# Heads in pairs on the contraction axis, and sread computed transposed

## The chip, the cores and the metric

The kernel runs on one core of a Trainium2 chip. The metric is device time in microseconds (us), lower is better. The core has five engines that run side by side, each through its own list of instructions in order: TensorE (PE in the profile, its weight loads PEld), VectorE (DVE), ScalarE (ACT), GpSimd (POOL) and SyncE (SP). POOL and SP start the DMA transfers here; the profile calls POOL's queue q0 and SP's queue q1.

## The reference

Cross attention between a long sequence x and 32 state rows, both ways, per batch and head, and then a feed-forward layer over all rows (B = 8 batches, H = 8 heads, S = 512, Ns = 32, D = 64, d_model = 512, d_ff = 2048):

```python
scores  = softmax(scale * x @ state^T)      # [B, H, 512, 32]
xread   = scores @ state                    # [B, H, 512, 64]
scores2 = softmax(scale * state @ x^T)      # [B, H, 32, 512]
sread   = scores2 @ x                       # [B, H, 32, 64]
x2 = concat([xread, sread], rows) -> [B * 544, H * D]
h  = x2 @ w_in
out = (h * sigmoid(h)) @ w_out              # float32 [4352, 512]
```

The inputs are float32; the kernel works in bf16 and sums in float32.

## The kernel before

Both softmaxes use the same exponentials, without a maximum: `exps` writes exp_nat = exp(scale * x state^T), with 128 sequence rows on the partitions and, in the free dimension, c (4 rows per partition), 4 heads ("slots") and 32 state rows. `norm` sums over the 32 on DVE, takes the reciprocal and multiplies on POOL (tile an). The xread rows are never formed: since xread @ w_in = a @ (state @ w_in), the kernel builds W1 = state @ w_in per head (`w1_cols`, L330) and G1 (L356) multiplies W1 with the transposed weights aT. ACT applies SiLU to the result (tile g, L377), and G2 (L385) multiplies g with w_out, 16 matmuls (ft) for each of four output blocks (tt). The sread rows of all batches are collected and put through w_in and w_out at the end as a ninth batch (L366, L385, L407).

Loading. x of a batch is [head, 512 rows, 64]. `fetch_x` loads it with one cast DMA from POOL (L99), partition p holding rows 4p to 4p+3 of each head: runs of 4 rows, 1 KB read and 512 B written in bf16. x_nat has ten blocks: block 0 and block 9 are ones, 1 to 8 are the heads. Two x_nat buffers exist, so the load of batch n+2 has to wait until sread of batch n has read its buffer. `transpose_x` (L111) makes xT by a DMA transpose from SP's queue; batches 0 and 1 use PE instead (`pe_transpose_x`, L187). The weights come in ten cast DMAs on POOL's queue (L116, L119), the state of batches 1 to 7 in one on the same queue (L200, tile st_b), issued after batch 0's norm. It is copied twice side by side (st_n, L462), transposed by PE in 16 pieces (L213) and evicted to stT in four copies.

Scores. The 128 contraction rows of one matmul hold two of the four c for one head. stT holds, for each head, a block of state for the upper and one for the lower 64 rows, with zeros elsewhere. A matmul has xT as the stationary operand and writes 2 x 32 columns (L238); a half batch (hg, four heads) takes 8 matmuls. The result is ordered slot, c, n, so `exps` reads it permuted.

Sread. `sread(b, hg)` (L289) takes exp_nat as stationary operand and five blocks of x_nat, four heads and the ones, as the moving one: 4 matmuls of 320 columns (L293). Only the diagonal blocks are of use, and the ones column gives the sum. DVE takes the reciprocal of one column (L302) and scales four 32x64 blocks into s_nat (L306). After batches 3 and 7 `transpose_s` turns s_nat into xmT by a DMA transpose.

Order of the work. It is written out by hand. In the loop for batch b = 1 to 7 the next batch n = b + 1 is prepared at fixed places (tt, ft) between the G2 matmuls: scores and exps of n at (0, 10) (at (0, 12) for b = 1), norm and the DMA transposes of a at (0, 14), sread at (1, 6) and (1, 13), `transpose_x(n + 1)` at (2, 12), W1 at (2, 8) and (3, 4), `load_x(n + 2)` at (3, 0). The first G1 of batch n stands at (3, 1). A DMA of POOL or SP starts as soon as its queue reaches it and its waits are met, whatever place it has between the matmuls. Batch 0 is different: its first part runs while weights and state arrive, with sread(0) at ft 8 and 9, the state at ft 3 to 5, the four column chunks of W1 at ft 0, 2, 6 and 10, and the PE transposes of x(1) at ft 14.

On SP the order per batch is: the two transposes of a, two stores, the transpose of x, two stores. PSUM: two banks each for G2 and G1, and four (a0 to a3, taken in turn by `bank`) for everything else.

Of the kernel before, what the change touches and what calls it, by code (L numbers as in the profile page):

```python
# [8 lines left out]
FP32 = mybir.dt.float32  # L9
BF16 = mybir.dt.bfloat16  # L10
# [7 lines left out]
B = 8  # L18
H = 8
# [10 lines left out]

HEAD_OF_SLOT = [[0, 1, 2, 3], [5, 4, 7, 6]]
# [3 lines left out]
def kernel(  # L35
# [15 lines left out]

    xpool = ctx.enter_context(tc.tile_pool(name="xpool", bufs=2))
    xtpool = ctx.enter_context(tc.tile_pool(name="xtpool", bufs=3))
# [18 lines left out]
    st_b = pers.tile([128, 16, D], BF16)  # L72
    st_n = pers.tile([128, 16, 2, D], BF16)
    st0_f = pers.tile([128, 2, D], FP32)
    st0_n = pers.tile([128, 2, 2, D], BF16)

    stT = pers.tile([128, B, H, 2, NS], BF16)
    w_in_sb = pers.tile([128, 4, DF], BF16)
    w_out_sb = pers.tile([128, NFT, DM], BF16)
    s_nat = pers.tile([128, 2, DM], BF16)  # L80
# [11 lines left out]
    def new_x(b):  # L92
        t = xpool.tile([128, 10, 4, D], BF16, tag="x_nat", name=f"x_nat{b}")
        x_nat[b] = t
        nc.gpsimd.memset(t[:, 0, :, :], 1.0)
        nc.gpsimd.memset(t[:, 9, :, :], 1.0)

    def fetch_x(b):
        nc.gpsimd.dma_start(  # L99
            x_nat[b][:, 1:9, :, :],  # L100
            x[b].rearrange("h (p c) d -> p h c d", p=128, c=4),
        )
# [5 lines left out]
    def transpose_x(b):  # L108
        t = xtpool.tile([128, 16, 128], BF16, tag="xT", name=f"xT{b}")
        xT[b] = t  # L110
        nc.sync.dma_start_transpose(  # L111
            t[:], x_nat[b][:, 1:9, :, :].rearrange("p h c d -> p (h c d)")
        )
# [14 lines left out]
    def keep_busy(n, pool, tag):  # L128
# [11 lines left out]
    nc.sync.dma_start(  # L140
        st0_f[:], state[0].rearrange("(g h) n d -> (h n) g d", g=2)
    )
# [7 lines left out]
    nc.vector.memset(stT[:, 1:8], 0.0)  # L150
    make_identity(nc, ident)
    new_x(0)
# [10 lines left out]
    for u in range(2):  # L163
        copy(nc.vector, st0_n[:, :, u, :], st0_f[:])
    ps0 = bank([128, 2, 4, NS], BF16, "ps_st0")
    for hg in range(2):
        nc.tensor.transpose(ps0[:, hg, :, :], st0_n[:, hg, :, :], ident[:])
    for u, eng in enumerate((nc.vector, nc.scalar)):
        copy(
            eng,  # L170
            stT[ds(64 * u, 64), 0, :, u, :],
            ps0[ds(64 * u, 64), :, :, :].rearrange("p g h n -> p (g h) n"),
        )
    keep_busy(3, psH, "h1")
# [4 lines left out]
    def pe_transpose_x(b, hg, nb=2, new=bank, engs=(nc.vector, nc.scalar)):  # L179
        if b not in xT:  # L180
            xT[b] = xtpool.tile([128, 16, 128], BF16, tag="xT", name=f"xT{b}")
        m = 8 // nb
        for u in range(nb):
            ps = new([128, m, 128], BF16, "ps_xt")
            for i in range(m):
                j = m * u + i
                nc.tensor.transpose(  # L187
                    ps[:, i, :],
                    x_nat[b][:, 1 + 4 * hg + j // 2, ds(2 * (j % 2), 2), :],
                    ident[:],  # L190
                )
            copy(engs[u], xT[b][:, ds(8 * hg + m * u, m), :], ps[:])

    copy(nc.vector, x_nat[0][:, 1:5, :, :], x_f[:, 0:4, :, :])
    pe_transpose_x(0, 0, 2, lambda sh, dt, nm: psO.tile(sh, dt, tag="o", name=nm))
    copy(nc.vector, x_nat[0][:, 5:9, :, :], x_f[:, 4:8, :, :])


    def load_state():
        nc.gpsimd.dma_start(  # L200
            st_b[:],
            state.rearrange("b h n d -> (b h n) d").rearrange("(p k) d -> p k d", k=16),
        )

    stT_v = stT.rearrange("p b h c (n2 k) -> p c b h n2 k", n2=2)
# [3 lines left out]
    def transpose_state(half):  # L209
        ps = bank([128, 8, B, H, 2], BF16, "ps_st")  # L210
        st_ps[half] = ps
        for kk in range(8):
            nc.tensor.transpose(  # L213
                ps[:, kk, :, :, :], st_n[:, 8 * half + kk, :, :], ident[:]
            )

    def evict_state(half, u, eng):
        dst = stT_v[
            ds(64 * u, 64), u, ds(1, 7), :, :, ds(8 * half, 8)
        ].rearrange("p b h n k -> p (b h) n k")  # L220
        src = st_ps[half][ds(64 * u, 64), :, ds(1, 7), :, :].rearrange(
            "p k b h n -> p (b h) n k"
        )
        copy(eng, dst, src)
# [7 lines left out]
    def scores(b, hg):  # L232
        ps = bank([128, 4, 4, NS], FP32, "ps_sc")
        sc_ps[hg] = ps
        for s in range(4):
            h = HEAD_OF_SLOT[hg][s]
            for cp in range(2):
                nc.tensor.matmul(  # L238
                    ps[:, s, ds(2 * cp, 2), :],
                    xT[b][:, 2 * h + cp, :],  # L240
                    stT[:, b, h, :, :],
                    start=True,
                    stop=True,
                    skip_group_check=True,
                )

    def exps(b, hg):
        e = att.tile([128, 4, 4, NS], BF16, tag="exp", name="exp_nat")
        exp_nat[b, hg] = e
        nc.scalar.activation(  # L250
            e[:],
            sc_ps[hg].rearrange("p s c n -> p c s n"),
            func=EXP,
            bias=0.0,
            scale=SCALE,
        )
# [32 lines left out]
    def sread(b, hg):  # L289
        e = exp_nat[b, hg]  # L290
        ps = bank([128, 5, D], FP32, "ps_sr")
        for c in range(4):
            nc.tensor.matmul(  # L293
                ps[:],
                e[:, c, :, :],
                x_nat[b][:, ds(5 * hg, 5), c, :],
                start=(c == 0),
                stop=(c == 3),
                skip_group_check=True,
            )  # L300
        rb = att.tile([128, 1], FP32, tag="rb", name="rb")
        nc.vector.reciprocal(rb[:], ps[:, 0 if hg == 0 else 4, 0:1])  # L302
        for s in range(4):
            h = HEAD_OF_SLOT[hg][s]
            blk = h + 1 - 5 * hg
            nc.vector.tensor_scalar(  # L306
                s_nat[ds(32 * (b % 4), 32), b // 4, ds(64 * h, 64)],
                ps[ds(32 * s, 32), blk, :],
                rb[ds(32 * s, 32), :],
                None,  # L310
                op0=MULT,
            )

    def transpose_s(q):
        nc.sync.dma_start_transpose(xmT[:, q, :, :], s_nat[:, q, :])
# [3 lines left out]
    def w1_cols(b, cols, engs):  # L319
        pss = {}  # L320
        if b not in W1:
            W1[b] = wpool.tile([128, 2, DF], BF16, tag="W1", name="W1")
        for f, n in cols:
            for hg in range(2):
                pss[f, hg] = bank([128, 512], FP32, "ps_w1")
            for s in range(4):
                for hg in range(2):
                    h = HEAD_OF_SLOT[hg][s]
                    r = 64 * (h % 2)
                    nc.tensor.matmul(  # L330
                        pss[f, hg][ds(32 * s, 32), 0:n],
                        stT[ds(r, 64), b, h, h % 2, :],
                        w_in_sb[ds(r, 64), h // 2, ds(f, n)],
                        start=True,
                        stop=True,
                        tile_position=(r, 32 * s),
                        skip_group_check=True,
                    )
        for f, n in cols:
            for hg in range(2):  # L340
                copy(engs[hg], W1[b][:, hg, ds(f, n)], pss[f, hg][:, 0:n])
# [95 lines left out]
    load_state()  # L437
# [17 lines left out]
    for ft in range(NFT):  # L455
# [4 lines left out]
        if ft == 3:  # L460
            for u in range(2):
                nc.vector.tensor_copy(st_n[:, :, u, :], st_b[:])  # L462
        if ft == 4:
            transpose_state(0)
            transpose_state(1)
            evict_state(0, 0, nc.vector)
            evict_state(0, 1, nc.vector)
            evict_state(1, 0, nc.vector)
        if ft == 5:
            evict_state(1, 1, nc.scalar)  # L470
        if ft in (8, 9):
            sread(0, ft - 8)
# [25 lines left out]
    for ft in range(NFT):  # L498
        if ft == 5:
            w1_chunks(1, (3,), (nc.scalar, nc.scalar))  # L500
        if ft == 9:
            sread(1, 0)
# [4 lines left out]
        if ft == 13:  # L507
            sread(1, 1)
            load_x(3)
# [6 lines left out]
    for b in range(1, B):  # L516
        n = b + 1
        lead = 4 if b == 1 else 6
        for tt in range(4):
            for ft in range(NFT):  # L520
# [3 lines left out]
                if n < B:  # L524
# [9 lines left out]
                    if at == (1, 6):  # L534
                        sread(n, 0)
                    if at == (1, 13):
                        sread(n, 1)
                        if n == 3:
                            transpose_s(0)
                        if n == 7:  # L540
                            transpose_s(1)
                    if at == (2, 12):
                        if n + 1 < B:
                            transpose_x(n + 1)
                    if at == (3, 0):
                        if n + 2 < B:
                            load_x(n + 2)
# [46 lines left out]
```

## Time and profile before

| | us |
|---|---|
| median of 3 runs | 236.28 (234.55, 236.28, 240.29) |
| the profiled execution, its own time | 236.61 |
| its span, first to last instruction | 234.70 |
| batch period in the middle (e.g. 77.7 to 101.8) | 24.07 |
| the period with the longest wait for aT (125.84 to 152.30) | 26.46 |

The span in 40 slices (one slice is 5.9 us) shows the load of each engine and of the DMA engines in tenths:

```profile
PE   7698899999989999999999959999999999999970
...
DVE  6626456702721183108410822136212721100110
ACT  3753669797287928691879257763977297544110
...
PEclk9999999999999999999999999999999999999996
...
DMA  6999991970493039603990296106410421110111
GB/s 194 182 209 204 204 137 50 185 129 3 55 226 125 0 46 199 182 0 47 185 174 0 45 186 130 45 3 160 110 45 3 113 89 47 45 44 36 57 26 63
```

A 9 for PE is a slice in which it has work nearly all the time; the low slices are the start, slice 24 (135 to 141 us) and the end. In the first five slices the DMA engines are full: weights, state and x(1) arrive. Of the two queues, q0 carries the casting loads of POOL, q1 the stores, the transposes and the first loads of SP. The row for PE in a slice says nothing of what it waits for; that is read from the chain and the waits. The clock granted to PE is full but for the end.

### The profile page before, as it was taken

What the parts mean: (1) busy time and instruction counts of PE and PEld (TensorE: products, weight loads), DVE (VectorE), ACT (ScalarE), POOL (GpSimd) and SP (SyncE); (2) the same over time, 40 slices, a digit from 0 to 9 for tenths busy, and PEclk for the clock granted to TensorE, in tenths of its full rate; (3) what the DMA queues carried; (4) which work ended last, traced back from release to release, by engine and by line L of the source; (5) the groups of instructions that cost most, each with busy time, mean ns of one, the idle gap of its engine ahead of it and who ended that gap; (6) DMA issues with size and microseconds to landing.
All of it is one profiled execution on the core that took longest, in us unless ns stands there. A gap on an engine that the chain in (4) does not pass through costs nothing.

```text
span 234.7 us, 3567 instructions
## 1 busy us (share of the span) xinstructions
PE 215.3 (92%) x1388; PEld 102.0 (43%) x1414; DVE 77.9 (33%) x184; ACT 141.2 (60%) x237; POOL 35.6 (15%) x56
## 2 busy tenths in 40 slices
PE   7698899999989999999999959999999999999970
PEld 2334335544434543444344424454345434566550
DVE  6626456702721183108410822136212721100110
ACT  3753669797287928691879257763977297544110
POOL 8670020400500050005000500021001200000000
PEclk9999999999999999999999999999999999999996
DMA  6999991970493039603990296106410421110111
GB/s 194 182 209 204 204 137 50 185 129 3 55 226 125 0 46 199 182 0 47 185 174 0 45 186 130 45 3 160 110 45 3 113 89 47 45 44 36 57 26 63
DMA packets 38637, 23.37 MB, mean 100 GB/s; under 512 B 21212, under 2 KB 34268, under 8 KB 38620
## 3 DMA queue, kind: packets, MB, share of 16 engines
q0 software_dynamic: 12192, 8.13, 25.8%
q1 hardware_dynamic: 26428, 15.01, 24.7%
q8 instruction: 11, 0.18, 0.3%
q14 instruction: 6, 0.05, 0.1%
HBM read 17.37 MB, written 8.91 MB: 112 GB/s over the span
## 4 chain that ended last, share of the span: by engine, by line
PE 68%; DMA 10%; ACT 8%; DVE 5%; issue 3%; POOL 1%; POOLq 0%; DVEq 0%
PE o L385 34%; DMA aT<-an 7%; DMA st_b<-in_state_dram 3%; PE ps_sr L293 3%; ACT g L377 2%; ACT L377 2%; PE ps_sc L238 2%; PE o_half L407 1%; DVE stT L125 1%; ACT exp_nat L250 1%; ACT o_sb L123 1%; POOL an L269 1%; DVE s_nat L306 1%; PE ps_xt L187 1%; DVE rs L266 1%
## 5 line engine op out<-in xcount | busy, mean ns | idle before, releaser
L385 PE MATMUL o<-w_out_sb,g 128*128 128x512 bf16 x488 | 135.0, 379 | 1.7 <-issue 0.8
L385 PEld LDWEIGHTS <-g 128*128 128x128 bf16 x528 | 49.8, 98 | 60.9 <-issue 10.6
L269 POOL TENSOR_TENSOR an<-exp_nat,rc 128x512 bf16<-128x512 bf16 (+1 forms) x16 | 15.9, 1008 | 131.6 <-DVE rc L267 131.6
L266 DVE TENSOR_REDUCE rs<-exp_nat 128x16 f32<-128x512 bf16 x16 | 10.6, 660 | 52.9 <-ACT exp_nat L250 52.9
L125 DVE COPY o_sb<-o 128x512 f32<-128x512 f32 x17 | 11.4, 669 | 46.3 <-PE o L385 46.3
L123 ACT ACTIVATE o_sb<-o 128x512 f32<-128x512 f32 x15 | 8.9, 597 | 29.3 <-issue 19.6
L306 DVE TENSOR_SCALAR s_nat<-ps_sr,rb 32x64 bf16<-32x64 f32 x64 | 18.0, 281 | 1.3
L250 ACT ACTIVATE exp_nat<-ps_sc 128x512 bf16<-128x512 f32 x16 | 8.8, 595 | 0.9 <-PE ps_sc L238 0.8
L293 PEld LDWEIGHTS <-exp_nat 128*128 128x128 bf16 x64 | 6.2, 98 | 5.2 <-ACT exp_nat L250 0.5
L366 PEld LDWEIGHTS <-w_in_sb 128*128 128x128 bf16 x64 | 6.3, 98 | 3.9
L250 ACT ACT_TABLE_LOAD x6 | 7.7, 1283 | 0.1
L377 ACT ACT_TABLE_LOAD x6 | 7.7, 1283 | 0.1
L330 PEld LDWEIGHTS <-stT 64*32 64x32 bf16 x264 | 2.8, 89 | 8.7 <-issue 8.5
L131 PE MATMUL ps_busy<-busy 128*128 128x512 bf16 x11 | 5.0, 584 | 1.3 <-DVE busy L148 1.2
L385 PE MATMUL o_a<-w_out_sb,g 128*128 128x512 bf16 x15 | 5.5, 379 | 0.1
L356 PEld LDWEIGHTS <-W_206 128*128 128x128 bf16 x32 | 2.8, 97 | 6.2 <-DVE W_206 L125 2.2
L356 PEld LDWEIGHTS <-W_2203 128*128 128x128 bf16 x32 | 3.1, 97 | 4.1 <-issue 0.8
L356 PEld LDWEIGHTS <-W_1932 128*128 128x128 bf16 x32 | 3.1, 97 | 4.1 <-issue 0.8
L356 PEld LDWEIGHTS <-W_1110 128*128 128x128 bf16 x32 | 3.1, 97 | 4.1 <-issue 0.8
L356 PEld LDWEIGHTS <-W_379 128*128 128x128 bf16 x32 | 3.1, 98 | 3.9 <-issue 0.3
L356 PEld LDWEIGHTS <-W_1384 128*128 128x128 bf16 x32 | 3.1, 98 | 3.8 <-issue 0.4
L356 PEld LDWEIGHTS <-W_835 128*128 128x128 bf16 x32 | 3.1, 98 | 3.7 <-issue 0.2
(520 smaller groups left out, 331.0 us busy)
## 6 DMA issues: line engine op xcount, KB each, us to landing
out_dram<-o_sb SPq DMA_DIRECT2D x33, 256.0 KB, 2.5
w_in_sb<-in_moe_w_in_dram POOLq DMA_DIRECT2D x3, 512.0 KB, 9.5
w_out_sb<-in_moe_w_out_dram POOLq DMA_DIRECT2D x3, 512.0 KB, 11.3
x_f<-in_x_dram SPq DMA_DIRECT2D x2, 512.0 KB, 4.7
w_in_sb<-in_moe_w_in_dram POOLq DMA_DIRECT2D x2, 256.0 KB, 6.8
w_out_sb<-in_moe_w_out_dram POOLq DMA_DIRECT2D x2, 256.0 KB, 7.2
x_nat_115<-in_x_dram POOLq DMA_DIRECT2D x1, 512.0 KB, 16.8
x_nat_225<-in_x_dram POOLq DMA_DIRECT2D x1, 512.0 KB, 5.8
```

Of the source, the lines that this page charges most:

```text
L123: nc.scalar.activation(dst, src, func=COPY, bias=0.0)
L125: eng.tensor_copy(dst, src)
L131: nc.tensor.matmul(ps[:], busy[:, 0:128], busy[:], start=True, stop=True, skip_group_check=True)
L250: nc.scalar.activation(e[:], sc_ps[hg].rearrange("p s c n -> p c s n"), func=EXP, bias=0.0, scale=SCALE,)
L266: nc.vector.tensor_reduce(rs[:], e[:], axis=AX, op=ADD)
L269: eng.tensor_tensor(a[:, ds(c, n)], e[:, ds(c, n)], rc[:, ds(c, n)].to_broadcast([128, n, 4, NS]), op=MULT,)
L293: nc.tensor.matmul(ps[:], e[:, c, :, :], x_nat[b][:, ds(5 * hg, 5), c, :], start=(c == 0), stop=(c == 3), skip_group_check=True,)
L306: nc.vector.tensor_scalar(s_nat[ds(32 * (b % 4), 32), b // 4, ds(64 * h, 64)], ps[ds(32 * s, 32), blk, :], rb[ds(32 * s, 32), :], None, op ...
L356: nc.tensor.matmul(ps[:], W1[b][:, hg, ds(128 * ft, 128)], aT[b][:, hg, :, :], start=(hg == 0), stop=(hg == 1), skip_group_check=True,)
L366: nc.tensor.matmul(ps[:, 0:256], w_in_sb[:, kt, ds(128 * ft, 128)], xmT[:, :, kt, :], start=(kt == 0), stop=(kt == 3), skip_group_check=True,)
L377: nc.scalar.activation(g[:, 0:n], ps[:, 0:n], func=SILU, bias=0.0)
L385: nc.tensor.matmul(outs[tt][:], gt[b * NFT + ft][:, ds(128 * tt, 128)], w_out_sb[:, ft, :], start=(ft == 0), stop=(ft == NFT - 1), skip_gr ...
```

## The change

Heads are taken in pairs on the contraction axis. x_nat becomes [partition, c, head, d] without the blocks of ones; a 128-row piece of xT then holds two heads of one c instead of two c of one head, and `exps` reads its scores in the order in which they lie. stT holds for each of the four head pairs two blocks of 32 columns; in heads 4 to 7 the two are swapped (`u ^ g`), which goes with HEAD_OF_SLOT in `w1_cols`.

- `fetch_x`: four DMAs, one for each c, with runs of 64 float32 (256 B) in memory, in place of one DMA with runs of 1 KB. x is loaded for batches 1 to 7 this way.
- State: seven float32 DMAs on SP's queue (runs of 256 B), two casts on DVE, 2 x 4 transposes, 2 x 4 evictions on DVE. A memset of one element on POOL, after batch 0's norm, holds the first of each group back.
- `sread(b)`: once per batch. A matrix of ones is the stationary operand of 8 matmuls over the exponentials (128 columns), which leaves the sums on all partitions; x_nat is the stationary operand of 16 matmuls (64 columns), which gives sread already transposed. DVE takes the reciprocal of 128 x 256 sums and multiplies four 64 x 64 pieces straight into xmT. s_nat and `transpose_s` go.
- Places: sread(0) from ft 8 and 9 to ft 3; sread(1) in one piece at ft 13; sread(n) from (1, 6) and (1, 13) to (1, 14); `load_x(n + 2)` from (3, 0) to (1, 14); `transpose_x(n + 1)` from (2, 12) to (1, 6). xtpool has two buffers instead of three.

In the new order SP has, per batch: the two transposes of a, one store, the transpose of x, three stores. On DVE the reciprocal and the four multiplies of sread(0) stand between the two casts of the state.

```diff
     def fetch_x(b):
-        nc.gpsimd.dma_start(
-            x_nat[b][:, 1:9, :, :],
-            x[b].rearrange("h (p c) d -> p h c d", p=128, c=4),
-        )
+        x_re = x[b].rearrange("h (p c) d -> p c h d", p=128, c=4)
+        for c in range(4):
+            nc.gpsimd.dma_start(x_nat[b][:, c, :, :], x_re[:, c, :, :])
...
-    def load_state():
-        nc.gpsimd.dma_start(
-            st_b[:],
-            state.rearrange("b h n d -> (b h n) d").rearrange("(p k) d -> p k d", k=16),
-        )
...
+    def load_state(q):
+        nc.gpsimd.memset(st_f[:, q, 0:1, 0:1], 0.0)
+        for i in range(1 if q == 0 else 0, 4):
+            nc.sync.dma_start(
+                st_f[ds(NS * i, NS), q], state[4 * q + i].rearrange("h n d -> n h d")
+            )
+
+    def cast_state(q):
+        copy(nc.vector, st_b[:, q], st_f[:, q])
...
     def scores(b, hg):
...
-        for s in range(4):
-            h = HEAD_OF_SLOT[hg][s]
-            for cp in range(2):
+        for c in range(4):
+            for j in range(2):
                 nc.tensor.matmul(
-                    ps[:, s, ds(2 * cp, 2), :],
-                    xT[b][:, 2 * h + cp, :],
-                    stT[:, b, h, :, :],
+                    ps[:, c, ds(2 * j, 2), :],
+                    xT[b][:, c, 2 * hg + j, :],
+                    stT[:, b, 2 * hg + j, :, :],
...
-    def sread(b, hg):
...
+    def sread(b):
+        ps = bank([128, 2, 4, 2, NS], FP32, "ps_sr")
+        for hg in range(2):
+            for c in range(4):
+                nc.tensor.matmul(
+                    ps[:, 1, ds(2 * hg, 2), :, :],
+                    ones[:],
+                    exp_nat[b, hg][:, c, :, :],
...
+        for kt in range(4):
+            for c in range(4):
+                nc.tensor.matmul(
+                    ps[:, 0, kt, :, :],
+                    x_nat[b][:, c, ds(2 * kt, 2), :],
+                    exp_nat[b, kt // 2][:, c, ds(2 * (kt % 2), 2), :],
...
+        rb = att.tile([128, 4, 2, NS], FP32, tag="rb", name="rb")
+        nc.vector.reciprocal(rb[:], ps[:, 1, :, :, :])
+        for g in range(2):
+            for u in range(2):
+                rows, k2 = ds(64 * u, 64), ds(2 * g, 2)
+                nc.vector.tensor_tensor(
+                    xmT[rows, b // 4, k2, ds(32 * (b % 4), 32)],
+                    ps[rows, 0, k2, u ^ g, :],
+                    rb[rows, k2, u ^ g, :],
+                    op=MULT,
+                )
...
         if ft == 3:
-            for u in range(2):
-                nc.vector.tensor_copy(st_n[:, :, u, :], st_b[:])
+            cast_state(0)
         if ft == 4:
+            cast_state(1)
             transpose_state(0)
+            evict_state(0, nc.vector)
+        if ft == 5:
             transpose_state(1)
-            evict_state(0, 0, nc.vector)
-            evict_state(0, 1, nc.vector)
-            evict_state(1, 0, nc.vector)
-        if ft == 5:
-            evict_state(1, 1, nc.scalar)
-        if ft in (8, 9):
-            sread(0, ft - 8)
+            evict_state(1, nc.vector)
+        if ft == 3:
+            sread(0)
...
                     if at == (1, 6):
-                        sread(n, 0)
-                    if at == (1, 13):
-                        sread(n, 1)
-                        if n == 3:
-                            transpose_s(0)
-                        if n == 7:
-                            transpose_s(1)
-                    if at == (2, 12):
                         if n + 1 < B:
                             transpose_x(n + 1)
-                    if at == (3, 0):
+                    if at == (1, 14):
+                        sread(n)
                         if n + 2 < B:
                             load_x(n + 2)
```

## The prediction

> **What bounds the kernel now.** I read four views in this order: busy times and chain shares, the chain in order of time, the waits, and the packets of each DMA queue in short windows.
>
> ```profile
> PE 215.3 (92%) x1388; PEld 102.0 (43%) x1414; DVE 77.9 (33%) x184; ACT 141.2 (60%) x237; POOL 35.6 (15%) x56
> ...
> PE 68%; DMA 10%; ACT 8%; DVE 5%; issue 3%; POOL 1%; POOLq 0%; DVEq 0%
> ```
>
> TensorE (PE) is the bound; the 10% of DMA is where it has to wait. From the chain in order of time (start, length):
>
> ```profile
> 11.39 7.37 DMA st_b<-in_state_dram
> 18.78 0.77 DVE st_n L462 x2
> ...
> 36.38 0.89 PE ps_xt L187 x16
> ...
> 126.97 0.47 PE ps_sc L238 x16
> ...
> 130.02 0.54 PE ps_sr L293 x4
> ...
> 133.14 7.28 DMA aT<-an
> ```
>
> Two places are not PE's own work: the state load that holds batch 0, and aT, the transposed weights that the first G1 of the next batch needs. The waits (total, times, longest, us) show the second one on PE:
>
> ```profile
> PE h_1702 L356 <- DMA aT<-an: 2.7, 1, 2.7
> ...
> PE h_879 L356 <- DMA aT<-an: 0.7, 1, 0.7
> ```
>
> With 0.3 at batch 4 (its first pair of G1 took 0.90 from start to end, the next 0.59) aT costs 3.7 us. Only batches 2 to 5 are exposed: behind their aT an x load starts. Batches 6 and 7, with no x load, never wait. Packet counts (packets, MB, share of 16 engines) in 28.5 to 30.5, in 136.1 to 138.5 and in 1.9 to 2.3 us:
>
> ```profile
> q0 software_dynamic: 775, 0.40, 145.4%
> ```
>
> ```profile
> q0 software_dynamic: 656, 0.34, 120.0%
> ```
>
> ```profile
> q1 hardware_dynamic: 242, 0.06, 64.7%
> ```
>
> First: an x load moves 775 packets of 1 KB read and 512 B written in 2.0 us, 41 ns per packet and engine, 2.6 us for its 1,024. Second: for 2.4 us the x load of batch 7 ran and SP's queue (q1), with stores and a transpose issued, got no packet; aT's semaphore came at 140.4, when that load landed (issued 133.29, 7.0 us). Third: 256 B rows of the first state load were busy 0.647 x 16 x 0.4 / 242 = 17 ns each.
>
> **PE work.** Sread now takes two blocks of 4 matmuls (0.54 each), 1.09 us a batch. It becomes 8 matmuls of 128 columns and 16 of 64, each with a new 128x128 weight. Nearest rows: 16 transposes of 128 columns in 0.89 us (56 ns each) and 16 scores of 64 columns in 0.47 (29 ns), both with a weight load each. So 8 x 56 + 16 x 29 = 0.92 us, -0.17 a batch, -1.4 over eight. Were each weight load to cost its 98 ns in full, 24 x 98 = 2.35 us and +10 in all; the scores, 16 loads in 0.47, exclude that. Scores stay 8 matmuls of 64 columns per half. State transposes fall from 18 to 12: 0.3 us, inside batch 0's waiting, taken as zero. So are the ACT exponential, whose 595 ns with a permuted read is what a plain 128x512 copy takes (597), the removed xmT transposes (1.9 and 1.2 us on SP, with nobody waiting) and POOL's removed memsets.
>
> **DVE per batch.** These groups (busy, mean ns) give the prices:
>
> ```profile
> L306 DVE TENSOR_SCALAR s_nat<-ps_sr,rb 32x64 bf16<-32x64 f32 x64 | 18.0, 281 | 1.3
> L267 DVE RECIPROCAL rc<-rs 128x16 f32<-128x16 f32 x16 | 4.0, 253 | 1.4
> L302 DVE RECIPROCAL rb<-ps_sr 128x1 f32<-128x1 f32 x16 | 2.6, 162 | 1.8 <-PE ps_sr L293 1.5
> ```
>
> Out go 8 x 281 + 2 x 162 = 2.6 us. In come four multiplies of 64 elements (281 each, 1.1) and a reciprocal of 256. That is 162 + 255 x (253-162)/15 = 1.7 us if the slope between the rows holds, 256 x 253/16 = 4.0 if the larger row scales whole. I take 2.3, nearer the slope, as both rows carry a fixed part: 3.4 us. Behind it on DVE stand the two W copies of tt 2, ft 8. PE reaches them 10 G2 (2.2 us) and one W block (0.5) after sread, and G1 needs the first copy 9 G2 (1.9) later. The copies start at most 0.7 late with 1.9 - 0.7 of room: zero. At 4.0 the cover is gone, about +1 in each of six batches. The Trainium skill (VectorE: DVE Perf Modes, "First, the fixed hardware budget") says the reciprocal runs its divide with a repeat count of 8; at the 0.96 GHz of its Specifications my estimate is 2.1 us, and the sum would be 0.2 us lower, all of it in batch 0.
>
> **Batch 0.** At the start the halved memset of stT (1.55 us) frees DVE up to 0.8 earlier for the cast of st0, but four evictions, at most 0.28 each, stand where DVE had one and ACT the other, ahead of the cast of x at 4.79: -0.8 to +0.8, taken as zero, since the two are alike in size. The state leaves POOL's queue for seven SP DMAs of 256 B rows, released by two tiny memsets after POOL's last an (11.44). SP took 0.45 to issue the like at 0.74, so they go out until about 15. Before, st_b landed at 18.8. If SP's queue is served at once, the second half lands 2.4 after issue (aT's median), at 17.4. If it is held by the saturated weight loads as SP's stores were in batch 4 (7.2 us from issue), 20 and 22. On DVE then: cast 0.47 (between 0.31 for 128x128 and 0.69 for 128x1024), sread(0) 3.4, cast 0.47, eight evictions at 0.28 (2.2), before the W copy for ft 6: 6.5 us. From 16.9, when DVE is free, W is copied at 24.1; from 20 at 27.2. Before, both W halves stood at 25.1. PE queues behind cast(1): state transposes, G2, all of the later W. PE has by then done sread(0), which it did at 27.4 and 28.6 before (already counted, with DVE's 2.6). So -1.0 to +2.1. I take +0.3: saturated q0 is the state in which these DMAs fall.
>
> **x loads.** Each x becomes four DMAs, 4,096 reads of 256 B writing 128 B in place of 1,024. POOL issues each in 0.94, 3.8 us a batch; next on POOL is an, 20 us later: hidden. Engine time is 4,096/16 x 17 ns = 4.4 us to 256 x 41 = 10.5. I take 22 ns, 5.6 us, because the 17 is for the same read size and the 41 sits at the byte rate (0.40 MB written, 0.80 read in 2.0 us), not at a packet rate. A rule against the change stands in the Trainium skill (DMA: Bandwidth & Descriptors, "Specifications"): below 512 B a DMA does read-modify-write. No run here shows 128 B writes; if it doubled the 22, an x load would take 11.3 us and the result be that of the last rival.
> The first consumer is batch 1: weights drain q0 at 28.2, so x(1) lands at 28.2 + 5.6 + 1 = 34.8 (33.6 to 39.7), wanted at 36.0 less what batch 0 gained: +0.4 (0 to +4). The load of x(2) is released by the earlier sread(0) but stands behind it, wanted by SP's transpose at 41.7, whose result scores need at 54: 12 us cover it.
> In batches 2 to 5 the load starts when POOL's an ends (108.8 in batch 4 for 109.2), beside the second aT. Counted from q0's first packet, aT landed after 2.9 (batch 2), under 2.4 (3), 2.8 (4) and 5.2 us (5): three times it slipped out while q0 ramped up, once it was held to the end of the load. G1 waits from about 2.5. The load now comes 0.4 earlier and keeps q0 full for 5.6 instead of 2.6 us, so I hold two of four to its end: 1.5 of ramp (135.2 to 136.7 in batch 5) and 5.6 less 2.5 is 4.6, less what sread saves PE and the earlier start cost, about 4.2 each; the other two wait 0.7. That is 9.8 for 3.7: +6.1. Bounds: -3.7 if the wait goes; all four held by a load of 10.5 us (1.5 + 10.5 - 2.5 = 9.5 each), +34; two, +17. The x transpose moves to (1,6); its 5 us of SP hold three stores back, which four o_sb buffers cover, and xT has until the next (0,10).
>
> **Sum.** -1.4 + 0.3 + 0.4 + 6.1 = +5.4. The profiled execution took 236.61 us (span 234.70 and 1.9 around it), 0.3 above the median, 236.28, of runs from 234.55 to 240.29. From the median: 241.7.
>
> **Rivals.**
> Little change: aT slips out as it does now, in all batches or all but one. 236.3 - 1.4 + 0.3 + 0.4 = 235.6 with today's 3.7, 238.8 with one more held. For it: three of four slip out now.
> Faster: POOL spreads the issue over 3.8 us, q1 finds gaps, aT lands 2.4 after its issue as in batches 6 and 7, and the state comes at 17.4: 236.3 - 1.4 - 1.0 - 3.7 = 230.2. It decides as soon as aT's tail takes less than 2.5 us from q0's first packet. Against: that packet comes 1.7 us after the issue, while aT is still being written.
> Much slower: packets at 35 to 41 ns. Place: aT in batches 2 to 5 (+9 with one held to a load's end, +17 with two) and x(1) at batch 1 (+4): 248 to 256; it parts from the forecast at about 28 ns, 7.2 us a load. Against: 17 ns at 256 B.
>
> **How the numbers follow.** Forecast 241.7, own range 239.5 to 245, chance 0.38; much slower 0.19; little change 0.20; faster 0.23. Leaving out the lower half of the faster case and the upper half of the much slower one gives 230 to 250. Two per cent, 231.6 and 241.0, is about what a measurement of this kernel can tell from no change. The faster case lies below 231.6: 0.23. Above 241.0 lie the much slower case and two thirds of the forecast: 0.19 + 0.26 = 0.45. That leaves 0.32.
>
> **What would show it.** PE: ps_sr matmuls in about 0.9 us a batch. DVE: rb at 2.3 us (1.7 to 4.0). q0: 4,096 packets per x, full for 5 to 7 us. Waits: PE for aT in batches 2 to 5, 5 to 12 us in total; for ps_xt of batch 1 at most 1. State landed before 20. No aT wait means the faster case; under 5 us, little change; x(1) after 38 the much slower one. A period above 24.07 us a batch with no such wait proves the PE or DVE price wrong.

## The result and the profile after

| | before | after |
|---|---|---|
| median of 4 runs, us | 238.28 (234.55 to 241.46) | 243.09 (242.84 to 244.65) |
| profiled execution, its span | 236.61, 234.70 | 242.84, 240.8 |

The changed kernel is slower: 1.034 times the time before, 95% interval 1.0242 to 1.0438. Two of the four runs before, 240.29 and 241.46 us, fell in a slower state that this kernel shows in some executions; the ratio leaves them out. The forecast of 241.7 us, +5.4, was near in size and had the sign: the two profiled executions differ by 6.2. Its main term, the wait for the transposed a, was wrong, and two terms held at or near nothing made up for it.

Busy time, share of the span and instructions of each engine, the granted clock in 40 slices, and the chain's shares, from the page of the changed kernel:

```profile
PE 218.7 (91%) x1509; PEld 104.3 (43%) x1536; DVE 77.6 (32%) x152; ACT 140.4 (58%) x235; POOL 50.0 (21%) x63
...
PEclk9769979999999999999999999999999999999997
...
PE 64%; DMA 12%; ACT 10%; DVE 8%; issue 2%; POOL 1%; SPq 0%; ACTq 0%; POOLq 0%; DVEq 0%
```

DVE went from 5 to 8% of the chain and DMA from 10 to 12%. PE's busy time rose by 3.4 us although sread got cheaper; the clock row shows why: it fell in slices 2, 3 and 6. The chain in order of time (start, length) has the milestones:

```profile
12.36 14.88 DMA w_out_sb<-in_moe_w_out_dram
27.53 7.74 DMA x_nat_237<-in_x_dram
...
43.05 0.89 PE ps_xt L186 x16
...
91.30 6.15 DMA aT<-an
...
110.44 0.47 PE ps_sc L248 x16
...
115.23 0.45 PE ps_sr L299 x8
115.67 0.48 PE ps_sr L309 x16
116.18 1.77 DVE rb L318
...
134.84 0.47 PE ps_sc L248 x16
```

The 12% for DMA are not the state: by the page they are the loads of w_out (6%) and of x(2) (3%), and aT (3%). In batch 0 the chain steps from PE to the load of x(2) at 35.27, though PE was idle for only 0.05 us from 32 to 36. Its releasers are inferred, so batch 0 is read from the waits.

The transposes of x(1) that end batch 0 stood at 36.38 and now stand at 43.05: +6.67, more than the whole difference of the spans (6.1). From there to the scores of batch 2 it is 18.15 against 18.20 before. The five periods to the scores of batch 7 take 122.45 (61.20 to 183.65) against 122.91 (54.58 to 177.49): -0.46. The rest, to the end of the span, is 57.15 against 57.21. So 6.67 - 0.05 - 0.46 - 0.06 = 6.1: the loss lies in batch 0, and batches 2 to 7 only come out even.

The waits of the changed kernel (total, times, longest, us) show what PE stood for, in batch 0 and later:

```profile
PE ps_st L221 <- DVE st_b L122: 6.4, 2, 4.7
...
DVE st_b L122 <- DMA st_f<-in_state_dram: 3.9, 1, 3.9
...
PEld L342 <- DVE xmT L322: 3.6, 6, 0.6
...
PE h_1201 L368 <- DMA aT<-an: 1.2, 1, 1.2
```

**Batch 0.** PE waits 6.4 us for the cast state. Before, its wait for the state's copy (st_n) was 1.0. The timeline of DVE and PE (start, length, operation, idle time before it and what ended it) shows the two casts and what PE did behind each:

```profile
22.34 0.43 DVE L122 CAST st_b<-st_f 128x512 bf16<-128x512 f32 x1 [3.89 <-DMA st_f<-in_state_dram]
...
28.91 0.43 DVE L122 CAST st_b<-st_f 128x512 bf16<-128x512 f32 x1 [3.51 <-issue]
...
29.39 0.61 PE L221 MATMUL ps_st<-ident,st_b 128*128 128x128 bf16 x4 [4.66 <-DVE st_b L122]
```

The second cast has "issue" as its releaser, which means that the trace names nobody; its data was the last of the state, whose DMAs took a median of 11.8 us from issue to landing. The last of them, issued at 14.5, took 14.3, so it landed at 28.8. Packets in 18 to 20 us (count, MB, share of 16 engines):

```profile
q0 software_dynamic: 310, 0.32, 92.7%
q1 hardware_dynamic: 312, 0.08, 29.7%
```

In this stretch the weights' queue q0 and SP's q1 move one packet each in turn, 155 a microsecond. A packet of q0 carries 1 KB, one of q1 256 bytes. The 7 x 256 = 1,792 packets of the state need 11.5 us at that rate: from about 15.5 to 27. Before, the state came in one transfer on q0. To the end of batch 0 PE was idle for 43.05 - 33.33 = 9.7 us (6.0 before) and busy for 33.33 (30.43 before): 3.8 more of idleness, and 2.9 more of work, which is nearly the same work at a lower clock (mean 0.88 up to there, 1.00 before).

The clock was 0.50 in two stretches, from 9 to 15.6 us and from 29.3 to about 32.7, right behind the wait of 4.66 us. By an estimate from these figures the second made 3.4 us of PE's work last 1.7 us longer than at the full clock. It goes with the state's wait. In all five kernels here in which PE stood 3.8 us or longer in one piece for the state (this one, and below sread(0) later, sread(n) earlier, half the bytes, and the fillers on the changed kernel) the clock fell to 0.50 late in such a wait or within 1 us of its end, for 3 to 14 us; in the others it was 1.00 from 24 to 40 us. The first stretch does not go with the state: three kernels below (the state on POOL's queue, half the packets, and one profile of the kernel before with the new x loads) have it with at most 1.1 us of waiting for the state.

**Steady state.** In the timeline of one batch, a W1 block (the matmuls that build W1) has three of its four PSUM banks (the tiles a0 to a3 that matmuls write in turn), and the weight load for the fourth waits until DVE has read sread's bank for the last time:

```profile
118.95 0.11 PEld L342 LDWEIGHTS <-stT 64*32 64x32 bf16 x7 [0.61 <-DVE xmT L322]
```

The groups (busy, mean ns of one, idle before) show what DVE does in that time, once a batch:

```profile
L318 DVE RECIPROCAL rb<-ps_sr 128x256 f32<-128x256 f32 x8 | 14.1, 1757 | 4.3 <-PE ps_sr L309 4.3
...
L322 DVE TENSOR_TENSOR xmT<-ps_sr,rb 64x64 bf16<-64x64 f32 x32 | 7.1, 222 | 0.6
```

That is 1.76 + 4 x 0.22 = 2.65 us in which sread's bank is not free. The four banks are taken in turn, so the fourth tile after sread's gets the same bank, and that is the last of this W1 block. Six times 0.6 is the 3.6 of the waits. Against it stand 2.5 us less waiting for aT (3.7 before, 1.2 now) and a cheaper sread.

**x loads.** In 32 to 34 us only x is loaded:

```profile
q0 software_dynamic: 2434, 0.31, 241.2%
```

2,434 packets in 2 us on 16 engines are 2 x 16 / 2434 = 13 ns each, counted as the 41 of the forecast was. The 17 was another measure, the busy time of one packet. By that measure these packets took 2.412 x 16 x 2 / 2434 = 32 ns, since more than two were in flight at once on an engine, so the 17 was no lower bound. By bytes the small packets are slower: 154 GB/s written in these 2 us, 199 for the x load of the kernel before at 28.5 to 30.5.

### The profile page after: what moved, and what is told of

The parts are those of the page before. It is cut to its first block, busy times and chain, and to the rows that moved or that the text cites. A ratio compares the mean times of both kernels' runs of the same rounds, so it can differ in the third digit from the quotient of the medians.

```text
span 240.8 us, 3799 instructions
## 1 busy us (share of the span) xinstructions
PE 218.7 (91%) x1509; PEld 104.3 (43%) x1536; DVE 77.6 (32%) x152; ACT 140.4 (58%) x235; POOL 50.0 (21%) x63
## 4 chain that ended last, share of the span: by engine, by line
PE 64%; DMA 12%; ACT 10%; DVE 8%; issue 2%; POOL 1%; SPq 0%; ACTq 0%; POOLq 0%; DVEq 0%
PE o L397 33%; DMA w_out_sb<-in_moe_w_out_dram 6%; DVE rb L318 4%; ACT g L389 3%; DMA x_nat_237<-in_x_dram 3%; ACT L389 3%; DMA aT<-an 3%; DVE xmT L322 2%; PE ps_sc L248 2%; PE o_half L419 1%; ACT o_sb L120 1%; PE ps_sr L309 1%; PE ps_busy L128 1%; PE ps_sr L299 1%; POOL an L273 1%
## 5 line engine op out<-in xcount | busy, mean ns | idle before, releaser
L318 DVE RECIPROCAL rb<-ps_sr 128x256 f32<-128x256 f32 x8 | 14.1, 1757 | 4.3 <-PE ps_sr L309 4.3
L342 PEld LDWEIGHTS <-stT 64*32 64x32 bf16 x264 | 3.4, 89 | 13.6 <-issue 9.4
L322 DVE TENSOR_TENSOR xmT<-ps_sr,rb 64x64 bf16<-64x64 f32 x32 | 7.1, 222 | 0.6
L221 PE MATMUL ps_st<-ident,st_b 128*128 128x128 bf16 x8 | 1.0, 265 | 6.4 <-DVE st_b L122 6.4
L397 PE MATMUL o_a<-w_out_sb,g 128*128 128x512 bf16 x16 | 6.4, 412 | 0.0
L98 POOL DMA_DIRECT2D x_nat_237<-in_x_dram x4 | 3.5, 874 | 9.7 <-DMA w_out_sb<-in_moe_w_out_dram 4.0
L368 PEld LDWEIGHTS <-W_207 128*128 128x128 bf16 x32 | 3.2, 103 | 5.3 <-DVE W_207 L122 1.7
L299 PEld LDWEIGHTS <-ones 128*128 128x128 bf16 x64 | 4.2, 98 | 1.9
L368 PEld LDWEIGHTS <-W_1731 128*128 128x128 bf16 x32 | 3.1, 98 | 4.1 <-issue 0.8
L368 PEld LDWEIGHTS <-W_2010 128*128 128x128 bf16 x32 | 3.1, 98 | 4.1 <-issue 0.8
L368 PEld LDWEIGHTS <-W_1447 128*128 128x128 bf16 x32 | 3.1, 98 | 4.2 <-issue 0.8
## 6 DMA issues: line engine op xcount, KB each, us to landing
st_f<-in_state_dram SPq DMA_DIRECT2D x8, 64.0 KB, 11.8
```

Source lines behind the costliest of these rows:

```text
L299: nc.tensor.matmul(ps[:, 1, ds(2 * hg, 2), :, :], ones[:], exp_nat[b, hg][:, c, :, :], start=(c == 0), stop=(c == 3), skip_group_check=True,)
L318: nc.vector.reciprocal(rb[:], ps[:, 1, :, :, :])
L322: nc.vector.tensor_tensor(xmT[rows, b // 4, k2, ds(32 * (b % 4), 32)], ps[rows, 0, k2, u ^ g, :], rb[rows, k2, u ^ g, :], op=MULT,)
L368: nc.tensor.matmul(ps[:], W1[b][:, hg, ds(128 * ft, 128)], aT[b][:, hg, :, :], start=(hg == 0), stop=(hg == 1), skip_group_check=True,)
L397: nc.tensor.matmul(outs[tt][:], gt[b * NFT + ft][:, ds(128 * tt, 128)], w_out_sb[:, ft, :], start=(ft == 0), stop=(ft == NFT - 1), skip_gr ...
```

## The experiments

Theory: batch 0 loses to the state, whose small packets share by turns with the weights, and each of six batches loses 0.5 to sread's bank. Rivals: the order on DVE, where sread(0) stands between the casts; the aT wait, as forecast; the lower clock as a cause of its own. Ratios are to the kernel before, on the same chip.

**The state issued at the start.** The memset that makes SP wait for POOL is left out.

```diff
     def load_state(q):
-        nc.gpsimd.memset(st_f[:, q, 0:1, 0:1], 0.0)
```

> The one-element memsets that hold the state DMAs back are left out, so SP issues them right behind the first loads of x, ahead of most weights; nothing else changes. Theory (the state's 256 B packets take turns one for one with the weights' packets, about 156 a us, so 1,792 of them take 11.5 us from 15.7 on): they now flow from 6 us, the first group lands before 14 and the second before 19, PE's two waits for the cast state (1.7 and 4.7 us) fall below 1 us together, 4 to 6 us off the changed kernel's 243 (about 238). Rival 1 (the reciprocal and multiplies of sread(0) between the two casts on DVE hold the state): waits stay, less than 1 us off. Rival 2 (what is lost is the half clock of PE at 9 to 15.6 us): the waits go but under 3 us of time come back, and the early state delays the first weights, so it may even lose.

Measured: 237.28 us (235.71 to 239.35), ratio 1.0023 (0.9974 to 1.0071). The transposes of x(1) start at 36.95, and the clock is full throughout. Its waits:

```profile
PE h L367 <- DMA aT<-an: 1.4, 1, 1.4
PE ps_w L341 <- DMA w_in_sb<-in_moe_w_in_dram: 1.4, 1, 1.4
...
PE ps_st L220 <- DVE st_b L122: 0.5, 1, 0.5
```

Removing the state from that stretch removes nearly the whole loss. One wait of 1.4 us for w_in is new. As the half clock went too, this run does not part it from the state; the state on POOL's queue, below, does.

**sread(0) later.** sread(0) no longer stands between the casts.

```diff
-        if ft == 3:
+        if ft == 8:
             sread(0)
```

> Only sread(0) is moved back from ft 3 to ft 8, so that on DVE its reciprocal (1.75 us) and four multiplies (0.93) stand behind both casts of the state and all evictions. Theory (the state lands late by its packets): the second cast still waits for its DMA until about 29 us, PE's second wait grows by the 0.9 us that sread(0) filled, total 243 to 245. Rival 1 (DVE order): the second wait falls by about 2.7 us and the total to 240 to 241.

Measured: 245.11 us (244.5 to 246.26), ratio 1.0383 (1.0308 to 1.0458). The wait did not shrink:

```profile
PE ps_st L221 <- DVE st_b L122: 7.1, 2, 3.8
```

The second cast, now with nothing of sread(0) ahead of it on DVE, starts no sooner (28.91 before this edit), and here the trace names its releaser:

```profile
29.37 0.43 DVE L122 CAST st_b<-st_f 128x512 bf16<-128x512 f32 x1 [6.49 <-DMA st_f<-in_state_dram]
```

With sread(0) away, PE has less to do while it waits, and the clock was half from 22 to 35 us. The order on DVE is not the cause.

**sread(n) earlier in the batch.** The bank is taken and freed six tiles sooner; the loads stay.

```diff
+                    if at == (1, 8):
+                        sread(n)
                     if at == (1, 14):
-                        sread(n)
                         if n + 2 < B:
```

> In batches 2 to 7 sread(n) is moved from (1, 14) to (1, 8); the x load keeps its place and is released by POOL's an as before. Theory (one PSUM bank is held by sread until the four multiplies end, and the second half of the first W block, which takes the same bank, waits 0.6 us on PE): that wait goes in all six batches, the period falls from 24.40 to about 23.9 us, 2 to 3 us off in all (about 240.5). Rival (the longer period is PE's own work, 24 weight loads instead of 8, or ACT): period stays above 24.3.

Measured: 240.99 us (240.13 to 243.04), ratio 1.0215 (1.0121 to 1.0309). The wait for xmT is gone, and the period is 23.90 (scores at 112.92, 136.82, 160.72, 184.62) in place of 24.40. The bank wait is shown, at 0.50 a batch; 2.6 us of aT waits (1.2 without the edit) and 5.5 for the state remain.

**The kernel before with the new x loads alone.**

```diff
-        nc.gpsimd.dma_start(
-            x_nat[b][:, 1:9, :, :],
-            x[b].rearrange("h (p c) d -> p h c d", p=128, c=4),
-        )
+        x_re = x[b].rearrange("h (p c) d -> p h c d", p=128, c=4)
+        for c in range(4):
+            nc.gpsimd.dma_start(x_nat[b][:, 1:9, c, :], x_re[:, :, c, :])
```

> The kernel before with each x load cut into four DMAs of 256 B runs, as the change has them, and nothing else. My forecast's step (packets four times as many hold aT's tail to the load's end in half of batches 2 to 5): aT waits of 8 to 12 us instead of 3.7, total 241 to 244. Theory after the result (13 ns a packet and the issue spread over 3.7 us make the load no longer, aT slips out): aT waits 0 to 4 us, total within 2 us of the kernel before.

Measured: 234.23 us (233.35 to 236.94), ratio 0.9909 (0.9858 to 0.996), and no wait for aT in the profile. A second time:

> The kernel before, with each batch's x loaded by four DMAs whose packets are 256 bytes read and 128 written, a second time, beside the corrected form of the changed kernel on the same chip. Theory (small packets take nothing, and the shorter transfers end the one wait of 2.7 us for the transposed a): 0.985 to 0.997 of the kernel before. Rival (the first result was a chance of one session): 0.997 to 1.01. If the two edits on the changed kernel give 234.7 us, this kernel and that one are within 1% of each other.

Measured: 236.3 us (233.74 to 239.67), ratio 0.9886 (0.9807 to 0.9964), with one wait for aT, of 1.1 us. The small packets of x cost this kernel nothing; both intervals lie below 1, so this part of the change is a small gain by itself, of about 1%. That is about what the waits for aT fell by (3.7 us before). Why the wait for aT differs between executions (none and 1.1 in the same kernel) is not settled.

**Both corrections together,** the early state and the earlier sread.

> Two edits on the changed kernel: the state's DMAs are issued at the start (the waiting memset is dropped), and sread(n) stands at feed-forward tile 8 of the second token block, with the next loads still at tile 14. Theory (the state's packets starved beside the weights, and a PSUM bank wait of about 0.6 us in each of six batches, are separate costs that add): the early issue took off 5.8 us and the earlier sread 2.1 to 3 us, so 243.1 - 5.8 - 2.6 = 234.7 us (233.5 to 236.0), with a period of 23.9 us and no wait on xmT over 1 us in all; that is about 1.5 to 4 us under the kernel before. Rival (each hides the other's time: what the earlier sread saves comes back as waits for the transposed a): 236.5 to 237.5 us, with aT waits of 3 us or more.

Measured: 234.85 us (233.73 to 238.66), ratio 0.9913 (0.9871 to 0.9956). The two add up, as the theory had it. The profiled execution, the longest of 13 (238.66 us), has the period of 23.90, 0.3 us of waiting for xmT, 2.5 for aT and 2.8 for w_in.

**The state through POOL's queue,** in two casting DMAs, transposed in pieces of 32. On that queue it stands behind the first six weight loads and ahead of the last four. The cut shows the loads alone.

```diff
-        for i in range(1 if q == 0 else 0, 4):
-            nc.sync.dma_start(
-                st_f[ds(NS * i, NS), q], state[4 * q + i].rearrange("h n d -> n h d")
-            )
+        b0 = 1 if q == 0 else 4
+        n = 3 if q == 0 else 4
+        nc.gpsimd.dma_start(
+            st_b[:, ds(b0, n)].rearrange("n b h d -> n (b h) d"),
+            state[b0 : b0 + n].rearrange("b h n d -> n (b h) d"),
+        )
```

> The changed kernel with the state loaded through POOL's queue, behind the weights of that stage, as two casting DMAs, and turned by 28 small transposes instead of 8 large ones. Theory (the state starves because its packets of 256 bytes on a second queue get one turn for each weight packet): in the weights' own queue it is served in order, so TensorE's two waits for st_b (6.4 us) are under 1 us, ps_xt of batch 1 starts by 38.5 us, and the time is 237 to 239.5 us (28 small transposes cost 1 to 2 us more). Rival (any load of the state in that stretch delays the weights by its bytes, whichever queue it is on): the waits move to w_in or w1 and the time stays at 241 us or more.

Measured: 234.91 us (233.57 to 237.15), ratio 0.9895 (0.9816 to 0.9974), better than expected. PE has no wait for the state at all, and x(1) is transposed from 36.34. The small packets are on the weights' own queue here, at the same place in the program. They pass in a row: q0 moved 1,840 packets under 512 bytes in 15 to 19 us, and the two DMAs landed 6.2 us after issue. So the loss was in the sharing between queues, not in the packets' size alone. The clock was half here too, from about 9 to 15 us, and yet the time is no longer than that of the kernel before: that stretch of half clock is not the changed kernel's loss.

**Half the packets, then half the bytes.** Only heads 0 to 3 of the state are read and used for all eight, in the first; only the first 32 elements of each row are read and used for all 64, in the second. The casts, changed to match, are not shown.

```diff
-                st_f[ds(NS * i, NS), q], state[4 * q + i].rearrange("h n d -> n h d")
+                st_f[ds(NS * i, NS), q, 0:4],
+                state[4 * q + i, 0:4].rearrange("h n d -> n h d"),
...
-                st_f[ds(NS * i, NS), q], state[4 * q + i].rearrange("h n d -> n h d")
+                st_f[ds(NS * i, NS), q, :, 0:32],
+                state[4 * q + i, :, :, 0:32].rearrange("h n d -> n h d"),
```

> The changed kernel with the state of heads 0 to 3 alone loaded for batches 1 to 7 (896 packets of 256 bytes in place of 1,792) and used for heads 4 to 7 as well; heads 4 to 7 of the state are left out, and the cast is made in two halves. Theory (SP's queue gets one packet for each packet of the weights' queue, about 156 a microsecond): 896 packets take about 5.8 us in place of 11.5, so they have landed by 21.5 to 22.5 us after a first packet at 15.5, the second cast starts at 23 to 25 us instead of 28.9, TensorE's waits for st_b are 0.5 to 2 us instead of 6.4, and the time is 237.5 to 239.5 us. Rival (the state waits for the weights to be through, whatever its size): the second cast stays at 28 us or later and the time at 242 to 244 us.

> The changed kernel with the first 32 elements alone of each row of the state loaded (1,792 packets of 128 bytes in place of 256) and used for the second 32 as well; the second half of each row is left out, and the cast is made in two halves. Theory (turns are taken by the packet, not by the byte): with as many packets as before the state lands no sooner, the second cast starts at 28 to 29.5 us, TensorE waits 5.5 us or more for st_b, and the time is 242 to 244.5 us. Rival (the two queues share by bytes): it lands like the run with half the packets, 237.5 to 239.5 us.

Measured with half the packets: 236.71 us (235.94 to 237.91), ratio 1.0109 (1.003 to 1.0188); with half the bytes: 241.88 us (239.96 to 242.44), ratio 1.0313 (1.0275 to 1.0351). The second pair of casts in the timeline, first with half the packets, then with half the bytes:

```profile
23.21 0.50 DVE L122 CAST st_b<-st_f 128x256 bf16<-128x256 f32 x2 [0.78 <-issue]
```

```profile
26.51 0.74 DVE L122 CAST st_b<-st_f 128x256 bf16<-128x256 f32 x2 [2.57 <-issue]
```

Half the bytes in as many packets leave 5.8 us of PE's wait; half the packets leave 1.1. With 128 bytes in a packet the queues still alternate, in 18 to 20 us:

```profile
q0 software_dynamic: 369, 0.36, 107.3%
q1 hardware_dynamic: 368, 0.04, 30.1%
```

A turn is shorter (184 a microsecond instead of 155), and so the cast came 2.4 us sooner than with full rows, where next to no change was expected. The number of turns follows the packets; the length of a turn follows the bytes a little. The rival of shares by bytes, with a landing like that of half the packets, is out.

**Filler matmuls** ahead of the first W1 columns.

```diff
+    keep_busy(4, psO, "o")
     w1_cols(0, [(0, 256)], (nc.scalar, nc.scalar))
```

> The changed kernel with four more filler matmuls on TensorE ahead of the first weight transposes, so that it does not stand idle while the first part of w_in lands (a gap of 0.5 us ahead of the half clock at 8.9 to 15.7 us in the profile). Theory (that half clock is the result of the gap, and cost 1.5 us): the clock is 1.00 at 10 to 15 us, the third tile's matmuls start 1.5 us earlier, but the state's wait takes the gain back, as its data land no sooner: 242 to 243.5 us. Rival 1 (the time comes through): 241 to 242 us. Rival 2 (the half clock has nothing to do with the gap): it stays, 243 to 244 us.

Measured: 244.01 us (241.93 to 245.19), ratio 1.0288 (1.0203 to 1.0373). The clock is 1.00 from 8 to 18 us, but x(1) is transposed from 45.68, with 7.2 us of waiting for the state and half clock from 30 to about 37: the time that the first tiles gained was lost again at the state, and more. The same fillers where nothing of the state is late:

> The changed kernel with the early issue of the state, sread(n) at tile 8, and the four filler matmuls ahead of the first weight transposes. Now nothing of the state waits behind that stage, so theory (the half clock there follows the idle gap, and its 1.5 us were hidden before by the state's wait) expects the gain to show: 232.5 to 234 us, against 234.85 without the fillers, with the clock at 1.00 from 8 to 16 us. Rival (the weights land no sooner, so TensorE only waits later): 234.5 to 236 us, with waits for w_in of 1.4 us or more at 15 to 18 us.

Measured: 234.64 us (233.85 to 236.15), ratio 0.9935 (0.9892 to 0.9979), the same as without them. The clock was full, and PE had no wait for w_in, which neither theory nor rival had; PE waited 2.3 us for aT. Over the two kernels the fillers bring nothing.

**The best of it,** the state on POOL's queue and sread(n) at tile 8.

> The changed kernel with the state on POOL's queue behind the weights, and sread(n) at tile 8 of the second token block. Theory (the two costs add, as they did with the early issue): 0.5 us less in each of six batches than the state on POOL's queue alone (234.9 us), less what the waits for the transposed a take back: 232 to 233.5 us, 0.975 to 0.985 of the kernel before, with a period of 23.9 us and the scores of batch 2 at 54 to 55 us. Rival (the two sreads' savings and the a waits cancel): 234 to 235.5 us, with a waits of 2.5 us or more.

Measured: 231.79 us (230.91 to 234.14), ratio 0.9836 (0.9755 to 0.9918): faster than both kernels, by less than 2% against the one before. The period is 23.90 and one wait for aT is left, of 0.3 us. Its page:

```profile
PE 213.2 (93%) x1529; PEld 102.8 (45%) x1556; DVE 76.4 (33%) x150; ACT 139.3 (61%) x235; POOL 50.5 (22%) x62
...
PEclk9999999999999999999999999999999999999996
...
PE 73%; ACT 10%; DVE 5%; DMA 4%; issue 3%; POOL 1%; SPq 0%; POOLq 0%; DVEq 0%
```

PE holds 73% of the chain (68% before), DMA 4% (10% before). Part of the step from the state on POOL's queue alone is the clock: that profile had half clock from about 9 to 15 us and transposed x(1) from 36.34, this one had none there and did so from 34.91.

## Why the prediction was right in size and wrong in its reasons

- **PE work, -1.4: right.** 0.45 + 0.48 a batch is what the prices of transposes and scores gave (0.92).
- **DVE per batch: the price was near, the place was missed.** 2.3 was taken for the reciprocal, near the slope; it took 1.76, the slope itself. A multiply took 222 ns, not 281. By the rule of the Trainium skill that was weighed (VectorE: DVE Perf Modes, "First, the fixed hardware budget") the estimate was 2.1; the measured 1.76 decides. The failing step is "The copies start at most 0.7 late with 1.9 - 0.7 of room: zero". It looked at the W copies behind on DVE, and not at the PSUM bank that sread holds until its last multiply. PE itself waits for that bank, with all of its queue behind it. The prediction's own figures would have shown it: DVE was to hold the bank for 3.4 us, and PE to be back at the W block 2.2 us after sread. The term was 0 and measured +0.5 to 0.6 a batch, 3.6 us of waits in all. The prediction's own sign of a wrong price, a period above 24.07 with no aT wait, came up (24.40).
- **Batch 0, "I take +0.3": the mis-sized term.** It measured +6.67. The landing was bounded by what an aT and a store had taken (2.4 and 7.2 us from issue), so at 20 and 22; it was 22.3 and nearly 29. Both rows were priced by the transfer, not by the packets. 1,792 packets, each behind one of the weights, are 11.5 us; that the state was seven DMAs of 256 B rows stood in the prediction, but was not used for it. The cast (0.43 for 0.47) was priced near enough; the runs with half the packets and half the bytes show which count decides. A page of the Trainium skill bears on this and was not used: DMA: Bandwidth & Descriptors, "Queues, rings and completion order", says that each engine takes the queues it has work for in turn, packet by packet. The 310 and 312 packets of the trace fit that. The page's packet is a group of descriptors, and no run here shows how it relates to a packet of the profile.
- **x(1), +0.4: nothing.** PE has no wait for x(1) in the list, as it came 6.7 us later than before.
- **x packets, 22 ns: too dear.** They took 13, so a load that was to last 5.6 us needs 4096/2434 x 2 = 3.4. The bounds, 17 and 41, mixed two measures, as said above. The doubling weighed with the rule of the Trainium skill (DMA: Bandwidth & Descriptors, "Specifications", read-modify-write below 512 bytes) does not show: by these packet counts the load takes 3.4 us against 2.6 with large packets, and the kernel before did not get slower with it (0.9909 and 0.9886).
- **aT, +6.1: wrong in sign, -2.5.** The failing step is "I hold two of four to its end". It was drawn from the one load that had held an aT to its end. The four issues are spread over 3.6 us by POOL. In 118 to 119 us q1 moved 504 packets beside q0's 157, in 119 to 120 only 36 beside 1,099: aT slipped out while the load started, as it did three times of four before. In batch 3 it did not: in 94 to 96 us q1 moved 60 packets beside q0's 2,132, the chain has 6.15 us for this aT, and PE waited its 1.2 us. So a full q0 can still hold aT, but it did so once, not twice, and at a cost of 1.2 us. Whether the spread of the issues helps is not shown; that the loads in four pieces do no harm to aT is, by the kernel before with these loads.
- **The rivals.** "Much slower" fell with the packet price. "Faster" was right about aT and the period's cover and wrong about the state. That the sum hit was luck: 8.6 too much for aT stood against 6.4 too little for batch 0 and 3.6 for the bank.

## What to carry to other kernels

Price a transfer that shares the DMA engines with another queue by its packets first, not its bytes: here rows of 256 bytes beside weights of 1 KB a packet got a fifth of the bytes, and the cures that worked were the other transfer's own queue and an earlier issue. When DVE work on a PSUM tile gets longer, count the banks: the next matmul that takes this bank in turn waits for the last read, even when DVE has room. A forecast whose sum is right says little; the waits by line show which of its terms was.

## What was not expected of the hardware

- While weights and state are loaded, the two queues alternate packet for packet, 310 to 312 with 256 bytes and 369 to 368 with 128 bytes in q1's packets. That is no rule for all stages: beside an x load q1 got 60 packets to q0's 2,132 (changed kernel, 94 to 96 us), and none to 656 (before, 136.1 to 138.5), with a transpose and stores issued. Why is open.
- PE's clock was halved for some us between 8 and 16 us in 4 of 14 profiled executions, the changed kernel's among them, and in one of two of the very same kernel (the one before with the new x loads). In the windows of the changed kernel (stretch, length, busy us and instructions of PE, PEld, DVE, ACT and POOL, then PEclk, DMA share, GB/s):

```profile
12.00:14.00 2.00, 1.95 (x6) 0.40 (x4) 0.62 (x2) 0.60 (x1) 2.00 (x4) 0.50 1.24 207
```

A pair of 128x512 matmuls of G1 took 1.05 us there (at 12.25), and 0.59 in the kernel before (at 12.62). What sets it off is open: both kernels with the fillers ran without it, but so did the best kernel, whose PE was busy for only 0.76 of the 2 us from 10 to 12. Between the two kernels with the state on POOL's queue, which do the same in batch 0, it went with 1.4 us.
